# Attention and two feed-forward blocks on one core: the causal mask as a VectorE addition in PSUM, fewer products for the row maxima, and a new order

## The chip, the cores and the metric

The kernel runs on one core of a Trainium2 chip. Its engines work side by side, each through its own queue in order: TensorE (PE; its weight loads are PEld), VectorE (DVE), ScalarE (ACT), GpSimd (POOL) and SyncE (SP), which here only issues DMA transfers. Matrix products go to PSUM, eight banks of 512 float32 columns on 128 partitions. The metric is the device time of one execution in microseconds, lower is better.

## The reference

Three steps, all in float32, for 2 batches of 448 tokens and 12 heads of 64:

```python
scores = scale * np.matmul(q, k.transpose(0, 1, 3, 2))        # scale = 1/8
mask = np.triu(np.ones((seq, seq), dtype=bool), k=1)
scores = np.where(mask, -1000000000.0, scores)
scores = scores - np.max(scores, axis=-1, keepdims=True)
attn = np.exp(scores)
attn = attn / (np.sum(attn, axis=-1, keepdims=True) + 1e-09)
x = np.matmul(attn, v)                                        # heads joined: 896 x 768

h = x @ w_in                                                  # 896 x 1024
e = np.exp(h - h_max); sm = e / (np.sum(e) + 1e-09)           # per token
solu = h * sm
ln = (solu - mean) / np.sqrt(var + 1e-06) * g_ln
x = ln @ w_out                                                # 896 x 768

h = np.maximum(x @ w_in2, 0.0)                                # 896 x 2048
out = h * h @ w_out2                                          # 896 x 768
```

## The kernel before

**Products in two parts.** Every operand of a product is split into a high part, rounded to the fast format of TensorE, and a low part, the rest. A product is then three: high x high, low x high, high x low.

**Attention, pair by pair.** The 24 heads are worked as 12 pairs, one head on partitions 0 to 63, the other on 64 to 127, so that two products of 64 rows stand side by side. For pair i the steps are named by a short name and i:

- `load_r`, `H`, `L`: keys and queries come in; ScalarE makes the high part, GpSimd the low part.
- `S0a`, `S0b`, `S0c`: products of queries and keys for the row maxima alone, in one group of 448 keys, one of 336 and 112, one of 224. VectorE adds the mask MK and reduces them (`mxa`, `mxb`, `mxc`, line 298), and so frees the banks.
- `mT`, `row`, `rowd`: TensorE turns the maxima into rows, ScalarE copies them out, and two DMA transfers put them into one row a head of the tile MR (lines 306 to 326).
- `Sa`, `Sb`: the transposed scores, keys on partitions, queries in columns, only at and above the diagonal. The first half tile has key block 0 (448 queries, at column 64) and key block 3 (64 queries, at column 0); the second has blocks 1 (320, at 192) and 2 (192, at 0). To the three products come the row maxima, subtracted as a product of NEG1 and MR, and the mask, four products of ID (halves of the identity) and TR (0 or -1e30), lines 348 to 353. Pair 0 subtracts its maxima in another way (line 359).
- `ea1`, `eb1`: ScalarE's exponential of a whole half tile, into PP.
- `Ua`, `Ub`: products of PP with the values and a column of ones; `EA`, `EB` copy them out.
- `sums`, `recips`, `rcd`, `spread`, `norm`: the sums go through DMA, a reciprocal on VectorE, DRAM and back as `bc`; GpSimd multiplies.
- `x_hi`, `x_lo`: the parts of x for the next product, high on ScalarE, low on VectorE.

**The weights.** w_in comes as 64-bit floats, put together by three integer operations of VectorE over 1024 columns (`wf.0` to `wf.5`, lines 150 to 152), then split: high part on ScalarE (`wh`), low part on VectorE or GpSimd (`wl`).

**PSUM.** Half score tiles take two of four banks (a tile is given back after its exponential); the products for the maxima, the transposed maxima and U share the other four. A step takes the bank that was given back the longest time ago in the written order, and waits for it.

**What sets the order.** The string SEQ lists all steps up to the second block; each engine gets its instructions in that order and keeps it. `fl` steps are products that nobody reads. Behind attention come the steps of the first block (`h0` to `h6`, the layer norm, `T`, `y0`, `y1`) and the second block, which is not in SEQ.

Of the kernel before, what the change touches and what calls it, by code (L numbers as in the profile page):

```python
# [31 lines left out]
load_r.5 mT.2 Sa.1 row.2 EA.0 rowd.2 EB.0 load_v.2 S0a.3 ea1.1 S0b.3 sums.0 mxa.3 Sb.1 lq.9 lq.2 mxb.3 S0c.3 Sa.2 H.4
mxc.3 eb1.1 L.4 S0c.4 mT.3 ea1.2 mxc.4 Sb.2 recips.0 row.3 lq.3 S0b.4 eb1.2 rcd.0 Ua.1 mxb.4 load_v.3 rowd.3 S0a.4
Ub.1 mxa.4 spread.0 wf.0 load_r.6 Ua.2 lq.7 EA.1 H.5 mT.4 Sa.3 row.4 EB.1 norm.0 sums.1 S0b.5 load_v.4 ea1.3 Ub.2
mxb.5 rowd.4 L.5 load_r.7 x_hi.0 recips.1 Sb.3 EA.2 rcd.1 EB.2 S0c.5 sums.2 S0a.5 H.6 mxc.5 Sa.4 mxa.5 eb1.3 L.6 S0a.6
spread.1 mT.5 Sb.4 recips.2 lq.10 row.5 mxa.6 ea1.4 rcd.2 rowd.5 S0b.6 x_lo.0 H.7 Ua.3 mxb.6 load_r.8 norm.1 S0c.6
Ub.3 mxc.6 L.7 x_hi.1 spread.2 S0b.7 Sa.5 eb1.4 mxb.7 EA.3 EB.3 S0c.7 mT.6 mxc.7 Sb.5 wh.0 sums.3 x_lo.1 row.6 wl.0
ea1.5 S0a.7 rowd.6 Ua.4 H.8 load_v.5 norm.2 recips.3 load_r.9 mxa.7 eb1.5 rcd.3 Ub.4 lq.11 wf.1 mT.7 EA.4 Sa.6
load_v.6 EB.4 row.7 sums.4 S0c.8 ea1.6 Sb.6 spread.3 rowd.7 L.8 mxc.8 S0b.8 H.9 Ua.5 mxb.8 load_v.7 x_hi.2 eb1.6
x_lo.2 Ub.5 recips.4 wh.1 norm.3 rcd.4 load_r.10 S0a.8 Sa.7 mxa.8 L.9 EA.5 spread.4 x_hi.3 mT.8 S0a.9 EB.5 Sb.7 mxa.9  # L40
row.8 sums.5 ea1.7 load_r.11 x_lo.3 S0c.9 Ua.6 H.10 rowd.8 mxc.9 norm.4 eb1.7 load_v.8 recips.5 S0b.9 rcd.5 Ub.6 mxb.9
ld.5 wl.1 x_hi.4 mT.9 EA.6 Sa.8 row.9 EB.6 x_lo.4 sums.6 S0a.10 ea1.8 Sb.8 spread.5 L.10 mxa.10 load_v.9 rowd.9 S0b.10
H.11 Ua.7 mxb.10 ld.3 norm.5 S0c.10 Ub.7 mxc.10 recips.6 rcd.6 wf.2 mT.10 EA.7 Sa.9 row.10 eb1.8 S0b.11 EB.7 Sb.9
x_hi.5 spread.6 ea1.9 sums.7 L.11 mxb.11 Ua.8 load_v.10 rowd.10 x_lo.5 S0a.11 Ub.8 mxa.11 norm.6 recips.7 rcd.7 S0c.11
Sa.10 mxc.11 ld.4 wf.3 EA.8 eb1.9 mT.11 Ua.9 row.11 ea1.10 rowd.11 Sb.10 x_hi.6 spread.7 wh.3 Ub.9 wh.2 eb1.10 wl.2
Sa.11 EB.8 x_lo.6 sums.8 load_v.11 Sb.11 norm.7 ea1.11 h0.0 recips.8 wf.4 rcd.8 EA.9 Ua.10 eb1.11 x_hi.7 EB.9 h0.1
spread.8 sums.9 x_lo.7 wh.4 h1.0 wl.3 Ua.11 recips.9 norm.8 rcd.9 Ub.10 wf.5 h1.1 x_hi.8 spread.9 h0.2 h1.2 wl.4 wh.5
h0.3 EA.10 x_lo.8 EB.10 wl.5 h1.3 sums.10 h0.4 norm.9 recips.10 Ub.11 rcd.10 h1.4 EA.11 x_hi.9 spread.10 EB.11 x_lo.9
h0.5 sums.11 h1.5 mx.0 h2.0 norm.10 ex.0 recips.11 mx.1 rcd.11 load_g.0 h2.1 mu.0 x_hi.10 h2.2 spread.11 x_lo.10 sq.0
de.0 h2.3 ex.1 va.0 pw.0 h2.4 mu.1 norm.11 h2.5 h3.0 mx.2 x_hi.11 h3.1 fa.0 de.1 ln.0 x_lo.11 h3.2 lw.0 ex.2 h3.3 sq.1  # L50
de.2 mu.2 h4.0 va.1 sq.2 h3.4 va.2 lw.1 of.0 T.0 pw.2 pw.1 h3.5 Th.0 h4.1 fa.2 mx.3 h4.2 fa.1 ex.3 Tl.0 lw.2 h4.3 ln.2
# [809 lines left out]
```

## Time and profile before

| what | us |
|---|---|
| runs: 469.32, 469.99, 470.15 | median 469.99 |
| the profiled execution | 469.13 |
| its span, first to last instruction | 467.3 |
| PE busy | 458.8 (98%) |
| DVE busy | 267.4 (57%) |
| ACT busy | 165.8 (35%) |
| POOL busy | 134.4 (29%) |

The profile is one execution. Attention takes about the first 100 us; the first h product stands in the chain at 101.7 us. Busy shares are means over stages that differ much, so the rows below are taken by stretch. The end of a matmul is modelled; how long a group of matmuls holds the engine is read from the start of one group to the start of the next, as the chain has it.

### The profile page before, as it was taken

The page shows a single profiled execution, that of the slowest core. Times are in us where ns is not written, and L with a number is a line of the kernel's source. Part 1 is how long each engine was busy: PE and PEld are TensorE (multiplying, and loading weights), DVE is VectorE, ACT ScalarE, POOL GpSimd, SP SyncE. Part 2 cuts the span into 40 slices and gives each one's busy share as a digit, 9 for nine tenths or more (in the row PEclk, how much of TensorE's full clock was granted, in tenths as well). Part 3 has the DMA queues.
Part 4 walks back from the last instruction along what each step waited for, and adds up shares of the span by engine and source line. Part 5 has one row for each costly group of instructions (what it writes and reads, how often), then busy time and mean ns, then how long its engine had stood idle before and what let it go on. Part 6 is the DMA issues. An engine that isn't in the chain of part 4 may idle for free.

```text
span 467.3 us, 6795 instructions
## 1 busy us (share of the span) xinstructions
PE 458.8 (98%) x2659; PEld 410.0 (88%) x2659; DVE 267.4 (57%) x514; ACT 165.8 (35%) x225; POOL 134.4 (29%) x95
## 2 busy tenths in 40 slices
...
GB/s 265 152 157 139 114 165 219 123 125 39 23 103 320 0 182 157 2 0 1 0 69 135 74 130 106 97 135 74 129 104 100 136 74 131 199 122 135 79 59 118
DMA packets 41713, 52.48 MB, mean 112 GB/s; under 512 B 18257, under 2 KB 32337, under 8 KB 41297
## 3 DMA queue, kind: packets, MB, share of 16 engines
...
q8 instruction: 21, 0.34, 0.3%
q14 instruction: 12, 0.09, 0.1%
...
## 4 chain that ended last, share of the span: by engine, by line
PE 92%; DVE 5%; issue 1%; DMA 1%; POOL 1%; ACT 1%; SPq 0%; DVEq 0%; ACTq 0%; POOLq 0%
PE h L775 25%; PE o L804 25%; PE y L641 12%; PE h L494 12%; PE U L377 8%; PE s L345 4%; DVE JK L298 2%; PE mxp L283 2%; PE T L619 1%; DMA bc<-d 1%; PE s L353 1%; DVE wf L151 1%; POOL x L419 1%; PE fill L523 1%; PE mT L306 0%
## 5 line engine op out<-in xcount | busy, mean ns | idle before, releaser
L697 POOL TENSOR_TENSOR w<-wf,w 128x768 fp32r<-128x768 f32 x32 | 59.2, 1851 | 207.4 <-ACT w L694 207.4
L775 PE MATMUL h<-yT,w 128*128 128x448 f32 x576 | 116.9, 365 | 0.0
L804 PE MATMUL o<-w,g 128*128 128x384 f32 x672 | 116.7, 336 | 0.0
L804 PEld LDWEIGHTS o<-w,g 128*128 128x128 f32 x672 | 116.5, 188 | 0.0
L775 PEld LDWEIGHTS h<-yT,w 128*128 128x128 f32 x576 | 108.2, 188 | 8.6
L694 ACT CAST w<-wf 128x768 fp32r<-128x768 f32 x32 | 26.8, 837 | 140.9 <-DVE wf L152 95.7
L150 DVE TENSOR_SCALAR wf<-raw 128x768 int32<-128x768 int32 (+1 forms) x46 | 27.7, 602 | 82.8 <-DMA raw<-in_moe_w_out_dram 57.4
L494 PE MATMUL h<-w,xT 128*128 128x512 f32 x252 | 59.2, 393 | 0.0
L641 PE MATMUL y<-lnT,w 128*128 128x384 f32 (+1 forms) x288 | 58.9, 365 | 0.0
L641 PEld LDWEIGHTS y<-lnT,w 128*128 128x128 f32 x288 | 51.9, 188 | 5.9
L494 PEld LDWEIGHTS h<-w,xT 128*128 128x128 f32 x252 | 46.9, 188 | 9.6
L298 DVE CUSTOM_DVE_ANT_0 JK<-mxp,MK 112x336 bf16<-112x336 f32 (+2 forms) x96 | 40.0, 446 | 24.8 <-PE mxp L283 21.3
L151 DVE SCALAR_TENSOR_TENSOR wf<-raw,wf 128x768 int32<-128x768 int32 (+1 forms) x46 | 51.2, 1112 | 1.6
L377 PE MATMUL U<-PP,VR 128*128 128x448 f32 (+1 forms) x192 | 48.6, 399 | 0.8 <-DVE mx L298 0.7
L152 DVE SCALAR_TENSOR_TENSOR wf<-raw,wf 128x768 int32<-128x768 int32 (+1 forms) x46 | 48.3, 1049 | 1.6
L377 PEld LDWEIGHTS U<-PP,VR 128*128 128x128 f32 x192 | 32.0, 190 | 16.1 <-issue 9.6
L419 POOL TENSOR_TENSOR x<-E,bc 64x448 f32<-64x448 f32 x24 | 30.5, 1270 | 40.8 <-DVE xT L431 23.3
L272 POOL TENSOR_TENSOR LO<-r,HI 128x896 fp32r<-128x896 f32 x12 | 26.9, 2245 | 14.6 <-ACT HI L268 14.2
L368 ACT ACTIVATE PP<-s 128x1024 f32<-128x1024 f32 x24 | 24.4, 1018 | 7.2 <-PE s L353 5.3
L761 DVE TENSOR_TENSOR relu<-h,relu 128x896 f32<-128x896 f32 x16 | 17.5, 1092 | 14.6 <-ACT relu L760 14.6
L389 ACT ACTIVATE E<-U,SE 128x448 f32<-128x448 f32 x24 | 14.6, 630 | 24.1 <-POOL x L419 15.1
L763 ACT CAST g<-relu 128x896 fp32r<-128x896 f32 x16 | 15.1, 941 | 18.6 <-DVE relu L761 18.6
...
## 6 DMA issues: line engine op xcount, KB each, us to landing
...
```

The lines of the kernel that those rows point to most:

```text
L150: nc.vector.tensor_scalar(xi, hw, 3, 0x3FFFFFFF, ALU.logical_shift_left, ALU.bitwise_and)
L151: nc.vector.scalar_tensor_tensor(xi, hw, -0x40000000, xi, ALU.bitwise_and, ALU.bitwise_or)
L152: nc.vector.scalar_tensor_tensor(xi, lw, 29, xi, ALU.logical_shift_right, ALU.bitwise_or)
L272: eng.tensor_tensor(LO[i % 3][:, :, 0:S], kq_raw.pop(i), f(HI[i % 3][:, :, 0:S]), ALU.subtract)
L298: nc.vector.tensor_tensor_reduce(JK[t], bs[h][0:JP, o : o + nk], MK[:, S - nk :], 1.0, NEG, ALU.add, ALU.max, mx[i][:, 4 * h + t : 4 * h + ...
L377: nc.tensor.matmul(UB[i][h][:, q0:S], VR[i % 3][:, t, h, :], PP[(2 * i + a) % NPP][:, h, o : o + nq], start=t == 0, stop=t == 2,)
L419: nc.gpsimd.tensor_tensor(x[D * h : D * h + D], e[0:D, h], bc[:, h], ALU.mult)
L494: nc.tensor.matmul(b[:, half, :], xT[c][s][:, t * P : t * P + P], W1[c][:, w, 512 * half : 512 * half + 512], start=(c == 0 and s == 0 and ...
L641: nc.tensor.matmul(b[:, ci, 0:n], WO[fi][:, w, c * P : c * P + P], M["lnT"][a][s][:, fi, :], start=(fi == 0 and w == 0 and s == 0), stop=( ...
L697: nc.gpsimd.tensor_tensor(W2[n][:, 1], w_f["2", n], f(W2[n][:, 0]), ALU.subtract)
L775: nc.tensor.matmul(b[:, a, 0:HT], W2[fi][:, w, c * P : c * P + P], yT[c][s][:, HT * a : HT * a + HT], start=(c == 0 and w == 0 and s == 0) ...
L804: nc.tensor.matmul(ob, G[fi + e][s][:, P * t : P * t + P], w, start=(fi + e == 0 and r == 0), stop=(fi + e == NF2 - 1 and r == 2),)
```

## The change

The four mask products of each half score tile are gone, and with them the tile ID. Instead VectorE adds the mask TR to the tile in PSUM, in place, before the exponential: a new step, `ka` for the first half (2 x 192 columns) and `kb` for the second (2 x 2 x 128 columns). The tile MR is 64 columns wider and holds the last 64 maxima of a head a second time in front of the others, so that the maxima of the first half are subtracted in one product of 512 columns a head; for that, `rowd` issues four transfers instead of two. All low parts of x are GpSimd's. PP has five buffers instead of four, one `fl` group is gone, and SEQ is written anew as a whole.

```diff
-NPP = 4
-XLO_POOL = ()
+NPP = 5
+XLO_POOL = (0, 1, 2, 3, 4, 5, 6, 7, 8, 9, 10, 11,)
...
 SEQ = """
-load_r.0 load_v.0 fl.0 fl.1 fl.2 H.0 load_r.1 fl.3 lq.4 load_v.1 L.0 S0c.0 S0a.0 fl.4 mxa.0 fl.5 mxc.0 fl.6 S0b.0 H.1
+load_r.0 fl.0 fl.1 fl.2 H.0 load_r.1 fl.3 lq.0 L.0 S0b.0 fl.4 mxb.0 fl.5 S0c.0 S0a.0 mxc.0 fl.6 H.1 load_r.2 fl.7
...
-            MR = [qk.tile([P, S], F32R, name=f"MR{i}") for i in range(3)]
+            MR = [qk.tile([P, D + S], F32R, name=f"MR{i}") for i in range(3)]
...
-            TR = per.tile([P, 2, 320], F32R, name="TR")
-            ID = per.tile([P, 2, P], F32R, name="ID")
+            TR = per.tile([P, D + P], F32, name="TR")
...
-                for h in range(2):
-                    nc.vector.tensor_copy(ID[D * h : D * h + D, j], ident[D * j : D * j + D])
-            nc.vector.tensor_copy(TR[D:P], f(TR[0:D]))
+            nc.gpsimd.memset(TR, 0.0)
+            for o, n in ((0, D), (D, P)):
+                ap = TR[:, o : o + n]
+                nc.gpsimd.affine_select(ap, ap, [[1, n]], ALU.is_ge, HUGE, base=0, channel_multiplier=-1)
...
                 for h in range(2):
                     nc.sync.dma_start(
-                        f(MR[i % 3][D * h : D * h + 1]).rearrange("o (t p) -> o t p", p=JP),
+                        f(MR[i % 3][D * h : D * h + 1, D:]).rearrange("o (t p) -> o t p", p=JP),
                         f(m2[4 * h : 4 * h + 4]),
                     )
+                    nc.sync.dma_start(f(MR[i % 3][D * h : D * h + 1, 0:D]), f(m2[4 * h + 3 : 4 * h + 4, JP - D :]))
...
-                for K, Q in ((HIk, HIq), (LOk, HIq), (HIk, LOq), (None, MR[i % 3])):
+                for K, Q in ((HIk, HIq), (LOk, HIq), (HIk, LOq)):
...
-                for j in range(2):
+                for o, x, n in () if i in mr else (((0, 0, D + S),), ((192, D + P, S - P), (0, D + 2 * P, S - 2 * P)))[a]:
                     for h in range(2):
                         r = slice(D * h, D * h + D)
-                        b = s[:, h, 0 : 192 * a + 192].rearrange("p (a c) -> p a c", c=192)[:, :, 0 : 192 - 64 * a]
-                        x = TR[r, j, 64 * a : 192 + 128 * a].rearrange("p (a c) -> p a c", a=1 + a)
-                        nc.tensor.matmul(b, ID[r, j], x, start=False, stop=j == 1 and i not in mr)
+                        nc.tensor.matmul(
+                            s[:, h, o : o + n], NEG1[r], MR[i % 3][r, x : x + n], start=False, stop=o == 0
+                        )
...
+            def causal(n):
+
+                if n % 2 == 0:
+                    x, y = sb[n][:, :, 0 : D + P], TR.unsqueeze(1).broadcast_to((P, 2, D + P))
+                else:
+                    x = sb[n][:, :, 0:384].rearrange("p h (b c) -> p h b c", c=192)[:, :, :, 0:P]
+                    y = TR[:, D:].unsqueeze(1).unsqueeze(1).broadcast_to((P, 2, 2, P))
+                nc.vector.tensor_tensor(x, x, y, ALU.add)
```

Three places show what stands on an engine now; line numbers of the changed kernel are a few higher or lower than those of the kernel before.

On TensorE, the first half score tile of pair 1 (HI and LO are parts of keys and queries, s is the tile), before:

```order
L345 MATMUL s<-LO_128,HI_125 128x448 x2
L345 MATMUL s<-LO_128,HI_125 128x64 x2
L345 MATMUL s<-MR_131,NEG_133 128x448 x2
L345 MATMUL s<-MR_131,NEG_133 64x64 x2
L353 MATMUL s<-TR,ID 128x192 x4
```

and in the changed kernel:

```order
L336 MATMUL s<-LO_128,HI_125 128x448 x2
L336 MATMUL s<-LO_128,HI_125 128x64 x2
L344 MATMUL s<-MR_131,NEG_133 128x512 x2
L300 MATMUL mT<-ident,mx 8x112
L379 MATMUL U<-PP_144,VR_140 128x320
```

The two products of the maxima (448 and 64 columns) are one of 512, the mask's four are gone, and the next step follows.

On VectorE, around the second conversion of w_in (`wf.1`, three operations on wf), from the last maxima of pair 7 (JK_139 is the 448-key group) to the next one, before:

```order
L298 ISA JK_139,mx<-mxp,MK 112x448
L298 ISA mx 112x1
L150 TENSOR_SCALAR wf<-raw 128x1024
L151 SCALAR_TENSOR_TENSOR wf<-raw,wf 128x1024
L152 SCALAR_TENSOR_TENSOR wf<-raw,wf 128x1024
L298 ISA JK_137,mx<-mxp,MK 112x224
L298 ISA mx 112x1
L298 ISA JK_137,mx<-mxp,MK 112x224
```

and in the changed kernel:

```order
L292 ISA JK_139,mx<-mxp,MK 112x448
L292 ISA mx 112x1
L151 TENSOR_SCALAR wf<-raw 128x1024
L152 SCALAR_TENSOR_TENSOR wf<-raw,wf 128x1024
L153 SCALAR_TENSOR_TENSOR wf<-raw,wf 128x1024
L367 TENSOR_TENSOR s<-s,TR 128x2x192
L292 ISA JK_139,mx<-mxp,MK 112x448
L292 ISA mx 112x1
L292 ISA JK_139,mx<-mxp,MK 112x448
L292 ISA mx 112x1
L367 TENSOR_TENSOR s<-s,TR 128x2x2x128
```

Behind the conversion now stand an addition of the mask (pair 6, first half), the 448-key maxima of pair 8 and a second addition, where the 224-key maxima of pair 8 stood.

On SyncE's queue, from the rows of maxima of pair 1 (MR_131) to those of pair 2 (MR_132; m holds the rows, raw is w_in, r keys and queries), before:

```order
L323 DMA MR_131<-m_338 1x4x112 x2
L478 DMA raw<-in_moe_w_in_dram 128x512 x2
L223 DMA r<-in_kq_dram 128x896
L323 DMA MR_132<-m_432 1x4x112 x2
L226 DMA VR_142<-in_v_dram 128x8x64
```

and in the changed kernel:

```order
L317 DMA MR_131<-m_338 1x4x112
L321 DMA MR_131<-m_338 1x16x4
L317 DMA MR_131<-m_338 1x4x112
L321 DMA MR_131<-m_338 1x16x4
L481 DMA raw<-in_moe_w_in_dram 128x512 x2
L224 DMA r<-in_kq_dram 128x896
L317 DMA MR_132<-m_398 1x4x112
L321 DMA MR_132<-m_398 1x16x4
L317 DMA MR_132<-m_398 1x4x112
L321 DMA MR_132<-m_398 1x16x4
```

Each pair's row transfers are four where there were two; what stands between them is the same here.

## Rows read from the trace of the kernel before

**Rows 1.** Busy us (x instructions) of each engine by stretch, TensorE's granted clock

```profile
12.00:99.00 87.00, 84.56 (x709) 65.70 (x707) 61.02 (x200) 47.70 (x71) 42.31 (x25) 1.00 0.54 156
99.00:464.00 365.00, 365.00 (x1916) 337.54 (x1912) 197.05 (x273) 113.36 (x149) 83.45 (x51) 1.00 0.31 96
```

**Rows 2.** Who TensorE waited for, 12 to 110 us: total, times, longest

```profile
PE mT L306 <- DVE mx L298: 1.0, 3, 0.5
PE U L377 <- DVE mx L298: 0.7, 1, 0.7
PE s L345 <- ACT PP L368: 0.6, 1, 0.6
```

**Rows 3.** Who VectorE waited for, 5 to 96 us: total, times, longest

```profile
DVE JK L298 <- PE mxp L283: 21.3, 19, 3.0
```

**Rows 4.** The chain that ended last: start us, length us, what (x instructions)

```profile
86.91 2.09 PE U L377 x8
...
89.60 1.92 PE U L377 x8
...
91.82 1.18 PE s L345 x16
...
98.77 1.37 PE s L345 x15
100.14 0.28 PE s L353 x4
...
101.47 0.25 PE s L353 x4
101.72 1.59 PE h L494 x6
...
121.64 20.42 PE h L494 x90
```

**Rows 5.** The timeline of the start: start us, us, engine, line, what [idle before]

```profile
3.85 0.87 DVE L254 CAST ID<-ident 64x128 fp32r<-64x128 f32 x4
...
4.73 0.49 DVE L255 CAST TR<-TR 64x640 fp32r<-64x640 f32 x1
...
6.86 0.56 DVE L298 CUSTOM_DVE_ANT_0 JK<-mxp,MK 112x448 bf16<-112x448 f32 x1
...
13.40 0.62 DVE L298 CUSTOM_DVE_ANT_0 JK<-mxp,MK 112x448 bf16<-112x448 f32 x1
...
14.85 0.26 PE L306 MATMUL mT<-ident,mx 112*8 112x112 f32 x1 [0.33 <-DVE mx L298]
```

**Rows 6.** VectorE by shape, 195 to 240 us: busy us, mean ns, idle before

```profile
L670 DVE TENSOR_TENSOR yT<-y,yT 128x512 fp32r<-128x512 f32 x6 | 4.2, 692 | 20.8 <-ACT yT L669 20.8
L670 DVE TENSOR_TENSOR yT<-y,yT 128x384 fp32r<-128x384 f32 x6 | 3.3, 557 | 3.3 <-ACT yT L669 3.3
```

**Rows 7.** VectorE by shape, 0 to 96 us: the low parts of x

```profile
L431 DVE TENSOR_TENSOR xT<-x,xT 128x448 fp32r<-128x448 f32 x6 | 5.0, 840 | 0.0
```

**Rows 8.** The timeline around two conversions of w_in

```profile
57.38 2.44 POOL L272 TENSOR_TENSOR LO<-r,HI 128x896 fp32r<-128x896 f32 x1
57.88 3.01 DVE L151 SCALAR_TENSOR_TENSOR wf<-raw,wf 128x1024 int32<-128x1024 int32 x1
...
92.72 0.69 DVE L150 TENSOR_SCALAR wf<-raw 128x1024 int32<-128x1024 int32 x1
...
93.44 1.23 DVE L151 SCALAR_TENSOR_TENSOR wf<-raw,wf 128x1024 int32<-128x1024 int32 x1
```

**Rows 9.** The timeline of the row of maxima and of small transfers

```profile
22.88 1.21 SPq L323 DMA_DIRECT2D MR<-m  x2
...
75.18 0.24 ACT L311 CAST m<-mT 8x112 fp32r<-8x112 f32 x1 [0.32 <-PE mT L306]
...
99.42 0.58 SPq L394 DMA_DIRECT2D sc<-E  x1
...
101.48 0.20 DVE L400 RECIPROCAL sr<-sc 112x8 f32<-112x8 f32 x1 [1.74 <-DMA sc<-E]
```

More of the change, by code (lines that the diff above doesn't have):

```diff
@@ L32 @@
[L32 to L51, printed above, removed]
@@ new lines @@
+mxa.0 load_v.0 fl.8 lq.1 L.1 S0c.1 fl.9 mxc.1 mxr.0 fl.10 S0a.1 S0b.1 mxa.1 Sa.0 mxb.1 H.2 load_r.3 L.2 ka.0 S0a.2
+mT.1 mxa.2 Sb.0 lq.2 row.1 ea1.0 rowd.1 lq.8 S0b.2 H.3 Ua.0 mxb.2 lq.3 L.3 load_r.4 kb.0 S0c.2 Sa.1 eb1.0 mxc.2 mT.2
+ka.1 Ub.0 row.2 rowd.2 ea1.1 load_v.1 S0a.3 EA.0 Sb.1 load_r.5 mxa.3 EB.0 sums.0 S0b.3 H.4 kb.1 S0c.3 Sa.2 mxc.3 eb1.1
+L.4 mxb.3 load_v.2 S0c.4 Sb.2 mxc.4 mT.3 recips.0 row.3 S0b.4 rcd.0 H.5 Ua.1 mxb.4 rowd.3 L.5 lq.4 ka.2 load_r.6 kb.2
+S0a.4 ea1.2 load_v.3 Ub.1 mxa.4 spread.0 eb1.2 wf.0 mT.4 EA.1 Sa.3 lq.5 row.4 EB.1 S0b.5 sums.1 Sb.3 Ua.2 mxb.5 H.6
@@ new lines @@
+load_v.4 rowd.4 norm.0 ka.3 recips.1 S0a.5 ea1.3 kb.3 Ub.2 rcd.1 load_r.7 mxa.5 x_hi.0 x_lo.0 S0c.5 EA.2 load_v.5 Sa.4
+mxc.5 eb1.3 spread.1 L.6 mT.5 S0c.6 Sb.4 row.5 mxc.6 EB.2 wh.0 ka.4 sums.2 S0a.6 Ua.3 rowd.5 mxa.6 ea1.4 lq.6 kb.4
+norm.1 H.7 S0b.6 recips.2 eb1.4 Ub.3 mxb.6 rcd.2 load_r.8 x_hi.1 wl.0 S0c.7 EA.3 Sa.5 EB.3 spread.2 x_lo.1 mT.6 sums.3
+ka.5 Sb.5 row.6 mxc.7 L.7 rowd.6 ea1.5 S0b.7 Ua.4 lq.7 mxb.7 norm.2 recips.3 kb.5 rcd.3 S0a.7 Ub.4 lq.9 mxa.7 eb1.5
+load_r.9 H.8 wf.1 mT.7 Sa.6 spread.3 row.7 EA.4 EB.4 S0a.8 x_hi.2 Sb.6 sums.4 load_v.6 x_lo.2 ka.6 Ua.5 rowd.7 H.9
@@ new lines @@
+mxa.8 norm.3 ea1.6 kb.6 S0c.8 Ub.5 recips.4 eb1.6 mxc.8 rcd.4 load_v.7 L.8 x_hi.3 S0b.8 Sa.7 EA.5 mxb.8 EB.5 wh.1
+sums.5 S0b.9 x_lo.3 mT.8 mxb.9 spread.4 Sb.7 row.8 load_r.10 L.9 rowd.8 S0a.9 ka.7 Ua.6 kb.7 load_v.8 ea1.7 recips.5
+mxa.9 rcd.5 eb1.7 norm.4 lq.10 Ub.6 H.10 load_r.11 S0c.9 Sa.8 wl.1 mxc.9 EA.6 spread.5 x_hi.4 EB.6 S0c.10 ka.8 mT.9
+lq.11 Sb.8 row.9 mxc.10 ea1.8 rowd.9 x_lo.4 S0b.10 Ua.7 sums.6 mxb.10 H.11 ld.3 L.10 kb.8 S0a.10 Sa.9 eb1.8 mxa.10
+norm.5 Sb.9 recips.6 ka.9 rcd.6 load_v.9 mT.10 Ub.7 row.10 load_g.0 wf.2 ea1.9 rowd.10 Ua.8 EA.7 spread.6 EB.7 x_hi.5
@@ new lines @@
+sums.7 kb.9 x_lo.5 ld.4 S0b.11 Ub.8 load_v.10 mxb.11 eb1.9 norm.6 S0a.11 Sa.10 mxa.11 recips.7 L.11 EA.8 S0c.11 rcd.7
+Sb.10 mxc.11 x_hi.6 mT.11 kb.10 Ua.9 row.11 EB.8 x_lo.6 rowd.11 ka.10 wh.2 spread.7 wf.3 ea1.10 sums.8 Ub.9 ld.5
+eb1.10 Sa.11 norm.7 recips.8 Ua.10 ka.11 rcd.8 load_v.11 ea1.11 Sb.11 wl.2 x_hi.7 EA.9 h0.0 EB.9 x_lo.7 kb.11 sums.9
+eb1.11 h0.1 spread.8 wf.4 wh.3 Ua.11 norm.8 recips.9 Ub.10 rcd.9 h1.0 wl.3 EA.10 spread.9 wh.4 h1.1 x_hi.8 EB.10 Ub.11
+x_lo.8 sums.10 norm.9 h0.2 recips.10 h1.2 rcd.10 wf.5 EA.11 EB.11 h0.3 x_hi.9 sums.11 h2.0 x_lo.9 wh.5 h1.3 recips.11
@@ new lines @@
+rcd.11 wl.4 spread.10 h3.0 wl.5 h1.4 h0.4 norm.10 h0.5 h1.5 mx.0 x_hi.10 spread.11 x_lo.10 h2.1 mx.1 ex.0 h2.2 mu.0
+ex.1 norm.11 h2.3 mu.1 sq.0 h2.4 de.0 va.0 x_hi.11 pw.0 h2.5 x_lo.11 h3.1 mx.2 lw.0 h3.2 de.1 ex.2 h3.3 mu.2 h3.4 fa.0
+ln.0 of.0 lw.1 h3.5 sq.1 T.0 h4.0 va.1 mx.3 pw.1 h4.1 fa.1 ex.3 h4.2 of.1 lw.2 Th.0 h4.3 oh.0 ln.1 ol.0 h4.4 sq.2 Tl.0
+h4.5 oh.1 mu.3 lw.3 h5.0 of.2 sq.3 T.1 h5.1 Th.1 mx.4 h5.2 ol.1 ex.4 lw.4 h5.3 de.2 de.3 va.2 h5.4 va.3 pw.2 mu.4 pw.3
+h5.5 fa.2 fa.3 ln.2 Tl.1 h6.0 sq.4 mx.5 T.2 ln.3 of.3 h6.1 ex.5 T.3 Th.2 h6.2 mu.5 oh.3 h6.3 l2.2 Tl.2 Th.3 l2.1 lw.5
@@ L57 @@
+oh.2 h6.4 Tl.3 sq.5 de.4 h6.5 de.5 ol.2 y0.0 mx.6 va.4 ex.6 of.4 y0.1 ol.3 oh.4 ol.4 y0.2 va.5 lw.6 mu.6 pw.5 l2.0
+pw.4 of.5 y0.3 de.6 oh.5 fa.4 of.6 lw.7 ln.4 y0.4 sq.6 fa.5 oh.6 ol.5 T.4 va.6 ol.6 pw.6 y0.5 Th.4 ln.5 Tl.4 fa.6 of.7
+ln.6 T.5 y0.6 Th.5 Tl.5 oh.7 ol.7 T.6 y0.7 Th.6 Tl.6 f2.0 y1.0 yo.2 g2.0 yo.1 o2.0 f2.1 y1.1 y1.2 yp.1 yp.0 g2.1 yo.0
 o2.1 yp.2
```

24 lines of the change are left out of this document (5 added, 19 removed).

## The prediction

> **What bounds the kernel now.** I read the views in this order: busy time by stretch, who waited for whom, the chain that ended last, then single rows around the score groups. From 99 to 464 us TensorE is busy all 365 us; from 12 to 99 us, where the attention pairs run, it is busy 84.6 of 87 us, at a granted clock of 1.00 in both [rows 1]. In that first stretch it waits for others about 2.3 us in all, nearly always for VectorE's maxima [rows 2]. So a microsecond of TensorE work that disappears is a microsecond of the span, as long as the engines that feed it keep up. VectorE is the one to watch: it is busy 61.0 of the same 87 us [rows 1], and most of its 26 us of idleness is 21.3 us of waiting for maximum products [rows 3], spare time before and something it can lose.
>
> **The change part by part, on TensorE.** The four mask matmuls behind each half score tile go. In the chain they hold the engine 0.28 us (first half) and 0.25 us (second half) from their first start to the next work [rows 4]; twelve of each are 12 x 0.28 + 12 x 0.25 = 6.4 us. They sit on the path, so I count all of it.
>
> In the first half the row of maxima was subtracted by 448 and 64 columns a head and is now one product of 512. No row shows a 512-column product on 64 rows. Four products cost 1.37 us in the first half (448 + 64) and 1.18 in the second (320 + 192), so 0.34 and 0.30 each; a 512-column product of the h stage takes 20.42 / 90 = 0.23 us [rows 4]. The saving is therefore between 0 (a single pair overlaps its weight loads no better) and 0.34 - 0.23 = 0.11 us; I take 0.06, the middle. Eleven pairs have it: 0.6 us, bounds 0 and 1.2.
>
> **The start.** VectorE no longer builds the identity halves and the second mask copy, 0.87 + 0.49 us in front of its first maximum at 6.86 us [rows 5]. From there to the first transposition, 14.85 us, it is the engine that TensorE ends up waiting for, and TensorE fills the time with products that nobody reads [rows 5]. So the chain moves up by 1.36 us, less 0.2 for the wider maxima tiles that it clears. I take 1.0 us; bounds 0 (if the first loads land no earlier and become what is late) and 1.4. The dropped filler group costs and saves nothing: it stood inside this wait.
>
> **What VectorE gets.** 24 additions in PSUM, of 384 and 512 elements. No row shows VectorE writing PSUM. The nearest rows read one PSUM and one SBUF operand at just these sizes and write SBUF: 0.56 and 0.69 us [rows 6]. From below, 384 of the 448 columns that a maximum pass reads from PSUM in 0.62 us [rows 5] are 0.53; from above, 0.84 is what an operation of 448 columns takes on average where others disturb it [rows 7]. I take the mean of the nearest rows, 0.62, 15.0 us in all (13 to 20). It gives up the low parts of x, 0.84 us each [rows 7], six of them within this stretch: 5.0 us. So VectorE has 61.0 + 15.0 - 5.0 = 71.0 us to do where TensorE, after the savings, has about 79. That fits, but only in the right order: 8 us of spare time where there were 26. What hides each addition is the distance on TensorE between a score tile and the U product that reads it: by the order, 6 to 13 us of TensorE work in every pair but the first, against 0.6 for the add and the exponential behind it.
>
> The cover is thin where VectorE converts w_in, because the additions and maxima queue behind three long operations. The second conversion is the clearest place. Between the maximum product for pair 7 (448 keys) and the product that needs the banks of pair 8's 448-key maximum, TensorE has a U half of 1.92, two score halves of 1.31 and 1.18, a U half of 2.09 and about 0.4 of small work: 6.9 us [rows 4]. VectorE has in that time one maximum (1.3 to 1.45 us from 13.40 to the transposition, [rows 5]), the conversion, an addition and another maximum. With an undisturbed conversion of 0.69 + 1.23 and, for the third operation, as much again, 3.15 us [rows 8], that is 6.4 us, no wait. With one of its operations stretched from 1.23 to 3.01, as [rows 8] has it, it is 8.2 us: a wait of 1.3 us. The first conversion has the same shape with a little less behind it, a wait of 0 to 1.2 us.
>
> **The low parts of x on GpSimd.** Twelve operations of some 1.2 us (half of a 2.44 us one on twice the columns, [rows 8]) on an engine with room. By themselves they cost nothing. What they may do is disturb VectorE: the middle operation of the second conversion starts at 57.88 beside a GpSimd operation that runs from 57.38 to 59.82, and ends 1.07 us after it, 3.01 us where the same operation undisturbed takes 1.23 [rows 8]. By the Trainium skill, page "SBUF — State Buffer", section "Who interferes with whom", this is a lock and not sharing: a VectorE instruction with two SBUF inputs and a GpSimd one that reads SBUF do not run together, the later waits the whole of the earlier out; one with at most one SBUF input is free of it. The trace agrees for the conversion. By that rule the additions, with one operand in PSUM, pay nothing, and each moved low part can hold up a conversion, which speaks against this half of the change.
>
> **The queue of row transfers.** The first 64 columns of the new maxima tile need a copy of their own: four transfers a pair where there were two. Each takes the queue 0.6 us (two in 1.21), and a small transfer is usable 2.06 us after its issue starts (99.42 to 101.48) [rows 9]. From the transposition to the copied row are 0.6 us (0.24 behind 0.32 of waiting), so the last of four is there 0.6 + 3 x 0.6 + 2.06 = 4.5 us after it. TensorE has, in the tightest three pairs (2, 9 and 11), 4.0 us of other work plus about 0.9 us of that tile's own products: 4.9. The cover holds by 0.4 us. Should something stand ahead in the queue, these pairs wait a few tenths.
>
> **Sum.** 6.4 + 0.6 + 1.0 = 8.0 us gained. For new waits at conversions, at the maximum products and at the tight pairs I take 2.0 us beyond the 2.3 there were; that is the middle of none (both conversions undisturbed) and 4 (both disturbed, 2.5, and half a microsecond in three pairs). Net 6.0 us. The profiled execution took 469.13 us (span 467.3 and 1.8 around it), which gives 463.1; the median of the runs lies 0.86 us above the profiled one, so 464.0 us. In the stages behind attention only the order changes, and TensorE never waits there now [rows 1].
>
> **Rivals.**
> 1. The conversions are hit: low parts on GpSimd land beside the conversions as the operation of 57.38 did, each of the four before the last score tile lasts 1.8 us longer, and half of this stands in TensorE's way beyond the forecast: 4 x 1.8 / 2 = 3.6 us, 467.6. (The page named above has this as a rule.) For it: [rows 8]. Against: leaving VectorE, the low parts also stop being blocked themselves (0.84 on average, where the add of 384 takes 0.56, [rows 6, 7]), and GpSimd had room before.
> 2. Slower: VectorE becomes the engine that sets the end of the attention stretch. It works in order, and its wait for products is 21.3 us [rows 3]; if those waits stay, since each product still waits for a bank that VectorE frees, it needs 71.0 + 21.3 = 92.3 us where the stretch took 87. That is 5.3 us more, less 1.0 from the start: about 474 us. It decides from 16 us of VectorE idleness on (71 + 16 = 87). Against: the waits in [rows 3] are largely those of an engine that is ahead, and they shrink as it has more to do.
> 3. The four row transfers come late: 22 more issues of 0.6 us are 13 us of the queue. If each of eleven pairs then waits 0.9 us, 10 us go and the result is 464.0 + 10 = 474 us, slower too. It needs the row copy or the queue to be about 1.3 us late in every pair; eight pairs have over 0.5 us more cover than the tight ones.
> 4. The additions replace the mask one for one (the change does not do what it says): TensorE, freed of 6.4 us, waits as long for the adds, and only start and merged product remain: 469.99 - 1.0 - 0.6 = 468.4. Against: the 6 to 13 us of cover.
>
> **How the numbers follow.** Forecast 0.62 (its own range 461 to 466.5), rival 1 0.17, rival 2 0.09, rival 3 0.04, rival 4 0.08. A measurement tells this kernel from no change at about 0.2%, 0.9 us: faster is below 469.1. The forecast, rival 1 and half of rival 4 lie there, 0.83; no difference is the other half, 0.04; slower are rivals 2 and 3, 0.13. The range for 8 in 10 reaches from 460.8 (no wait at all, the start's upper bound) to 469.0, which takes in rivals 1 and 4.
>
> **What would show it.** The mask matmuls gone and the 512-column product at about 0.28 us a pair; the first transposition near 13.7 us; the additions at 0.56 and 0.69; the first h product some 6 us earlier than 101.7 [rows 4]. Wrong would be: TensorE waits for VectorE or ScalarE over 6 us in the attention stretch, conversions of 5 us and more throughout, or score tiles waiting for a transfer of the maxima row. A wait in the stages behind would mean that their order, which I took as harmless, is not.

## The result, and the profile after

The changed kernel is slower: 476.51 us (four runs, 474.63 to 478.71) beside 469.65 for the kernel before (469.09 to 470.15), a ratio of 1.0148 [1.0102, 1.0194]. The forecast was 464.0, range 460.8 to 469.0: wrong in its sign. The profiled execution took 478.71 us, its span is 476.9, 9.6 more than before, and its mean granted clock is 0.981 where it was 1.000.

The stretches of the changed kernel, as in [rows 1]: busy us (x instructions) of PE, PEld, DVE, ACT, POOL, then the granted clock, DMA share and GB/s.

```profile
12.00:99.00 87.00, 81.00 (x568) 60.39 (x567) 59.24 (x209) 43.89 (x63) 43.83 (x30) 0.92 0.52 138
99.00:464.00 365.00, 362.46 (x1884) 332.54 (x1882) 198.50 (x273) 116.62 (x153) 93.62 (x59) 1.00 0.32 99
```

The same by shorter stretches:

```profile
12.00:40.00 28.00, 27.70 (x216) 20.99 (x213) 20.25 (x79) 13.46 (x19) 8.19 (x4) 1.00 0.49 130
40.00:60.00 20.00, 17.42 (x101) 12.57 (x102) 12.59 (x45) 9.59 (x14) 13.15 (x10) 0.74 0.40 104
```

Read the first line of this block and then the second: up to 40 us nothing is wrong, from 40 to 60 TensorE is idle 2.58 us and, worse, runs at a mean clock of 0.74. TensorE is idle 6.0 us from 12 to 99 us where it was 2.4, and 2.5 us behind 99 where it was 0. Over the whole span the idle time is 476.9 - 462.8 = 14.1 us against 467.3 - 458.8 = 8.5: 5.6 more. The clock costs, by an estimate from its mean, 476.9 x (1 - 0.981) = 9.1 us. Together 14.7, of which 9.6 are seen; the rest, 5.1, is by this estimate work that really went. So in this execution nearly two thirds of what was lost are not waits at all, they are what follows the waits. It is the longest of the four: the other three, at mean clocks of 0.989, 0.993 and 0.993, took 476.58, 474.63 and 476.44 us, and by the same estimate the clock cost them 5.2, 3.3 and 3.3 us. So the waits weighed more there.

Who TensorE waited for, 12 to 130 us (total, times, longest), against [rows 2]:

```profile
PE mxp L277 <- DVE mx L292: 4.9, 6, 2.4
PE h L497 <- ACT E L391: 1.9, 1, 1.9
PE s L344 <- DMA MR<-m: 1.0, 1, 1.0
PE mT L300 <- DMA raw<-in_moe_w_in_dram: 0.7, 1, 0.7
```

And VectorE in the same stretch, against [rows 3]:

```profile
DVE JK L292 <- PE mxp L277: 17.1, 15, 2.8
DVE sr L402 <- DMA sc<-E: 16.0, 7, 7.7
```

TensorE waits for VectorE's maxima, while VectorE is only busy 59 us of 87. VectorE is not overloaded; it stands at line 402, the reciprocal of the sums, waiting for a transfer: 16.0 us, where the kernel before has 4.2 in the same view. This is the row to follow, but not by its total. Nearly half of it is one long wait near the end, and a faster kernel of the experiments below, e1, has it too (changed kernel, then e1):

```profile
123.31 0.20 DVE L402 RECIPROCAL sr<-sc 112x8 f32<-112x8 f32 x1 [7.66 <-DMA sc<-E]
...
111.66 0.20 DVE L402 RECIPROCAL sr<-sc 112x8 f32<-112x8 f32 x1 [8.02 <-DMA sc<-E]
```

The total less this longest wait is 8.3 us here, and 7.0 in e13, 4.3 in e5, 3.5 in e1 and 2.2 in e9: the order of their times.

The transfer of the sums of pair 1 starts in SyncE's queue at 35.16 us (start, length of the issue):

```profile
29.38 0.67 SPq L317 DMA_DIRECT2D MR<-m  x1
30.11 0.56 SPq L321 DMA_DIRECT2D MR<-m  x1
30.71 0.62 SPq L317 DMA_DIRECT2D MR<-m  x1
31.38 0.52 SPq L321 DMA_DIRECT2D MR<-m  x1
...
35.16 0.55 SPq L396 DMA_DIRECT2D sc<-E  x1
```

The queue has no pause there: nine issues stand end to end from 29.38 us to the sums, and the four row transfers take 2.37 us of that. The chain that ended last runs through them, and then through 5.79 us of the sums' transfer. The sums are used 5.8 us after their issue starts, and this is what VectorE and TensorE then do (start, length, idle before and its releaser):

```profile
40.98 0.20 DVE L402 RECIPROCAL sr<-sc 112x8 f32<-112x8 f32 x1 [3.58 <-DMA sc<-E]
41.10 0.67 DVE L367 TENSOR_TENSOR s<-s,TR 128x512 f32<-128x512 f32 x1
41.68 0.61 DVE L292 CUSTOM_DVE_ANT_0 JK<-mxp,MK 112x448 bf16<-112x448 f32 x1
...
42.36 0.55 PE L277 MATMUL mxp<-HI 64*128 64x224 f32 x1 [2.39 <-DVE mx L292]
```

VectorE waits 3.58 us for the sums with an addition of the mask and the 448-key maxima queued behind; these maxima hold the PSUM bank that TensorE wants next, and TensorE is idle 2.39 us. Its clock afterwards, in stretches around that moment (columns as above):

```profile
38.00:40.00 2.00, 1.97 (x10) 1.35 (x8) 0.00 (x0) 0.95 (x2) 0.00 (x0) 1.00 1.13 205
40.00:42.00 2.00, 0.00 (x0) 0.00 (x0) 1.02 (x3) 0.00 (x0) 1.89 (x2) 1.00 0.39 67
42.00:44.00 2.00, 1.42 (x8) 1.15 (x9) 1.52 (x7) 1.60 (x3) 1.32 (x2) 0.54 0.67 181
44.00:48.00 4.00, 4.00 (x29) 3.37 (x29) 1.28 (x7) 2.11 (x4) 2.80 (x3) 0.50 0.56 148
...
52.00:54.00 2.00, 2.00 (x11) 1.30 (x11) 0.79 (x5) 0.60 (x2) 1.32 (x2) 0.90 0.78 212
```

Until 42 us it is granted 2.4 GHz; from then, after an idle stretch of two microseconds, 1.2 GHz, for ten microseconds of nearly unbroken work (48 to 52 us reads as 44 to 48), before it rises again. So a wait of 2.4 us cost about 5 more behind it (half of ten, an estimate). There are two more such places, of which this is the next:

```profile
63.69 0.69 DVE L151 TENSOR_SCALAR wf<-raw 128x1024 int32<-128x1024 int32 x1 [1.55 <-DMA raw<-in_moe_w_in_dram]
...
65.68 2.05 DVE L153 SCALAR_TENSOR_TENSOR wf<-raw,wf 128x1024 int32<-128x1024 int32 x1
...
68.79 0.37 PE L277 MATMUL mxp<-HI 64*128 64x224 f32 x1 [1.40 <-DVE mx L292]
```

At 63.69 a conversion waits 1.55 us for its weights, another late transfer, its third operation takes 2.05 us where the second took 1.23, and then TensorE waits for the maxima behind it. At 126.32 the first block's products wait (the second row of TensorE's waits, 1.9 us) for a PSUM bank that ScalarE's copy of U frees, and the copy for a buffer that GpSimd's multiplication frees. From there the chain that ended last goes back over GpSimd's other work, two low parts of x among it (1.73 and 1.12 us), and two `bc` transfers to the row transfers of the last pair, 101.65 to 103.63. But e1 and e9 have 0.8 and 1.0 us of the same wait, so the added transfers are not all of it.

### The profile page after: what moved, and what is told of

The parts are those of the page before. It is cut to its first block, busy times and chain, and to the rows that moved or that the text cites. A ratio compares the mean times of both kernels' runs of the same rounds, so it can differ in the third digit from the quotient of the medians.

```text
span 476.9 us, 6621 instructions
## 1 busy us (share of the span) xinstructions
PE 462.8 (97%) x2539; PEld 409.2 (86%) x2539; DVE 268.1 (56%) x521; ACT 166.6 (35%) x225; POOL 144.4 (30%) x103
## 4 chain that ended last, share of the span: by engine, by line
PE 82%; DMA 6%; POOL 4%; SPq 4%; issue 2%; ACT 1%; DVE 1%; ACTq 0%; POOLq 0%; DVEq 0%
PE h L778 24%; PE o L807 24%; PE y L644 12%; PE h L497 10%; PE U L379 3%; DMA bc<-d 2%; POOL x L421 2%; PE s L336 2%; PE fill L526 2%; PE mxp L277 1%; SPq L317 1%; PE T L622 1%; DMA d<-sr 1%; DMA sc<-E 1%; SPq L321 1%
## 5 line engine op out<-in xcount | busy, mean ns | idle before, releaser
L497 PE MATMUL h<-w,xT 128*128 128x512 f32 x252 | 61.1, 401 | 1.9 <-ACT E L391 1.9
L497 PEld LDWEIGHTS h<-w,xT 128*128 128x128 f32 x252 | 47.9, 192 | 12.3 <-ACT E L391 2.3
L379 PE MATMUL U<-PP,VR 128*128 128x448 f32 (+1 forms) x192 | 51.6, 417 | 0.0
L152 DVE SCALAR_TENSOR_TENSOR wf<-raw,wf 128x768 int32<-128x768 int32 (+1 forms) x46 | 47.3, 1029 | 1.6
L153 DVE SCALAR_TENSOR_TENSOR wf<-raw,wf 128x768 int32<-128x768 int32 (+1 forms) x46 | 47.3, 1028 | 1.6
L379 PEld LDWEIGHTS U<-PP,VR 128*128 128x128 f32 x192 | 33.7, 200 | 16.8 <-issue 11.8
L421 POOL TENSOR_TENSOR x<-E,bc 64x448 f32<-64x448 f32 x24 | 29.0, 1208 | 28.8 <-DMA bc<-d 27.9
L266 POOL TENSOR_TENSOR LO<-r,HI 128x896 fp32r<-128x896 f32 x12 | 25.2, 2100 | 16.0 <-ACT HI L262 15.8
L277 PE MATMUL mxp<-HI 64*128 64x336 f32 (+3 forms) x96 | 17.0, 366 | 4.9 <-DVE mx L292 4.9
```

What stands on the lines that cost most here:

```text
L152: nc.vector.scalar_tensor_tensor(xi, hw, -0x40000000, xi, ALU.bitwise_and, ALU.bitwise_or)
L153: nc.vector.scalar_tensor_tensor(xi, lw, 29, xi, ALU.logical_shift_right, ALU.bitwise_or)
L379: nc.tensor.matmul(UB[i][h][:, q0:S], VR[i % 3][:, t, h, :], PP[(2 * i + a) % NPP][:, h, o : o + nq], start=t == 0, stop=t == 2,)
L421: nc.gpsimd.tensor_tensor(x[D * h : D * h + D], e[0:D, h], bc[:, h], ALU.mult)
L497: nc.tensor.matmul(b[:, half, :], xT[c][s][:, t * P : t * P + P], W1[c][:, w, 512 * half : 512 * half + 512], start=(c == 0 and s == 0 and ...
```

## Experiments

Theory Q: the 22 added row transfers delay everything that SyncE issues behind them (sums, weights, keys and queries), and VectorE, in order, passes the delay on. Rivals: the additions load VectorE too much (V); GpSimd's low parts are the harm, to VectorE or by GpSimd's own lateness (G; the recorded expectations call it P); the new order as a whole is bad (O). In e4 and e13 the added copies go to columns that nobody reads, and e14 adds part of the mask twice, which leaves the result as it is. Comparisons with e1 and with the changed kernel are of medians; the kernel before had 469.36 to 469.65 beside them.

### e1_two_rows: two row transfers a pair, the rest as changed

```diff
-MR = [qk.tile([P, D + S], ...
+MR = [qk.tile([P, S], ...
-nc.sync.dma_start(f(MR[i % 3][D * h : D * h + 1, 0:D]), f(m2[4 * h + 3 : 4 * h + 4, JP - D :]))
-s[:, h, o : o + n], NEG1[r], MR[i % 3][r, x : x + n]           # one product of 512
+s[:M, h, o : o + nq], NEG1[r, 0:M], MR[i % 3][r, q0 : q0 + nq]  # 448 and 64
```

> The changed kernel with two row transfers a pair and the row subtracted by 448 and 64 columns again; order, additions and GpSimd's share stay. Theory Q (22 more transfers crowd the transfer queue, so sums and loads come late, VectorE stands at the reciprocal and TensorE's clock falls): VectorE's 16.0 us of waiting for sums falls under 6, time 467 to 470. Theory O (the new order itself puts the sums behind bulk loads and the reciprocals ahead of additions): waits stay over 12 us, time 474 to 478. Theory P (GpSimd's low parts): as O, 474 to 478.

465.52 us, 0.9915 [0.9900, 0.9930]: 11 us faster than the changed kernel and 4 faster than the kernel before. Its clock is 1.00 in every stretch. The same place in it: the rows take two issues, the sums leave 1.64 us earlier, and TensorE waits 0.80.

```profile
28.60 1.31 SPq L317 DMA_DIRECT2D MR<-m  x2
...
33.52 0.59 SPq L396 DMA_DIRECT2D sc<-E  x1
...
39.15 0.20 DVE L402 RECIPROCAL sr<-sc 112x8 f32<-112x8 f32 x1 [2.21 <-DMA sc<-E]
...
40.53 0.37 PE L277 MATMUL mxp<-HI 64*128 64x224 f32 x1 [0.80 <-DVE mx L292]
```

The added transfers, with the one product of 512 columns that they served, are the cause of the sign. The additions, GpSimd's low parts and the new order are still in this kernel and it is faster. It came out better than Q had expected (467 to 470), while VectorE's wait for the sums stayed at 11.5 us and did not fall under 6: 8.0 of it is the long wait near the end.

### e13_three_rows: e1 with one added transfer a pair

```diff
+if h == 0:
+    nc.sync.dma_start(f(MR[i % 3][0:1, S:]), f(m2[3:4, JP - D :]))
```

> The kernel with two row transfers a pair and one more on SyncE's queue (a copy of 64 maxima that nobody reads): three transfers. Theory Q, each 0.6 us of issue in front of sums and loads counts by itself: half of the way from 465.5 to 476.5, so 468 to 473. Rival: the loss comes at a step, only where several delays meet: 465 to 467, all of it with the fourth transfer.

471.74 us, 1.0046 [1.0023, 1.0069], 6.2 above e1 where two added transfers cost 11.0. TensorE's idle time from 12 to 130 us is 6.7 us (3.8 in e1, 8.6 with two), the clock 0.91 from 40 to 60 us (0.74 with two). VectorE's wait for the sums is 16.0 us as with two added, and shows the dose only without the longest wait (7.0, between 3.5 and 8.3). So the loss grows with each transfer, and not through the product, since nobody reads the copy.

### e4_before_four_rows: the kernel before with the two added transfers

```diff
+nc.sync.dma_start(f(MR[i % 3][D * h : D * h + 1, 0:D]), f(m2[4 * h + 3 : 4 * h + 4, JP - D :]))
```

> The kernel before with two more row transfers a pair (the second copy of the last 64 maxima is written and not read); all else as before. Theory Q: each costs 0.6 us of the queue in the tight pairs, 472 to 477 with clock dips. Theory O: 469 to 471, the queue has room in that order.

474.40 us, 1.0110 [1.0091, 1.0129]: 5 us, without any of the other edits. The path is another one here: the reciprocals' way back (`bc`) is late for GpSimd, whose multiplication frees the buffer that ScalarE copies U into, whose PSUM bank TensorE wants.

```profile
83.03 3.25 POOL L420 TENSOR_TENSOR x<-E,bc 64x448 f32<-64x448 f32 x2 [3.47 <-DMA bc<-d]
...
86.32 0.63 ACT L390 ACTIVATE E<-U,SE 128x448 f32<-128x448 f32 x1 [7.05 <-POOL x L420]
...
87.00 0.47 PE L283 MATMUL mxp<-HI 64*128 64x336 f32 x3 [1.76 <-ACT E L390]
```

### e5_rows_on_act and e9_all_rows_on_act: rows issued by ScalarE

e5 is the changed kernel with its two added transfers issued by ScalarE, e9 is e1 with both row transfers there:

```diff
-nc.sync.dma_start(f(MR[i % 3][D * h : D * h + 1, ...
+nc.scalar.dma_start(f(MR[i % 3][D * h : D * h + 1, ...
```

> The changed kernel with the two extra row transfers a pair issued from ScalarE's queue instead of SyncE's; four transfers and the 512-column product stay. If it is the issue time on SyncE's queue that delays sums and loads (theory Q): 465 to 470, VectorE waits for sums under 13 us. If it is the transfers themselves (more small packets in the DMA engines): 474 to 478 as in the changed kernel. If ScalarE has no room for 1.2 us of issues a pair: over 470 with TensorE waiting for exponentials.

> The kernel with two row transfers a pair (465.5 us), both issued from ScalarE's queue right behind the copy of the row; SyncE's queue loses another 1.2 us a pair. If the queue is still what makes the sums late: VectorE's wait for sums under 8 us, 462 to 464.8. If what is left is the time the bulk loads take in the DMA engines: 465 to 467, VectorE's wait about 11.5 us as now.

e5: 467.40 us, 0.9953 [0.9938, 0.9967]. The same 44 transfers, the same bytes, half of them on another queue, and 9.1 us less: of the 11.0 that e1 gains, most is the place in SyncE's queue and not the transfers themselves. The 1.9 us that e5 stays above e1 (467.40 and 465.52) can be the transfers or their issue by ScalarE. e9: 464.68 us, 0.9894 [0.9877, 0.9912], the lowest median and ahead of both kernels; its interval overlaps that of e1, so the 0.8 us between the two are not shown. VectorE's wait for the sums is 10.5 us, not under 8 as expected, 8.3 of it the long one. All that TensorE waits for in it, 12 to 130 us:

```profile
PE h L497 <- ACT E L391: 1.0, 1, 1.0
PE mxp L277 <- DVE mx L292: 0.4, 2, 0.2
```

### e10_rows_sums_on_act: e9 with the sums issued by ScalarE too

```diff
-nc.sync.dma_start(c, ee[i][D : D + 1] ...
+nc.scalar.dma_start(c, ee[i][D : D + 1] ...
```

> As the kernel before it, and the transfers of the sums too from ScalarE's queue, so that none of them stands behind bulk loads in SyncE's queue. If the queue position is what is left: under 464. If ScalarE's 1.8 us a pair of issues, in order in front of its exponentials, cost more than they save: 466 to 470.

470.53 us over all ten runs, which reach from 467.6 to 475.9; the ratio, 1.0020 [1.0003, 1.0037], leaves out the two longest. Worse than e9, not better. Its profile is of the longest run, so I read no cause from it. It stays open.

### e6_recips_later and e7_sums_first: two cures by order

e6 is the changed kernel with `recips` of pairs 0 to 8 (and `rcd`, in part `spread`) three VectorE steps later; e7 is e1 with bulk loads put behind the sums, pairs 0 to 5. Around pair 0 in e6, pair 1 in e7 (steps of SEQ; "..." stands for steps that stay):

```diff
-mT.3 recips.0 row.3 S0b.4 rcd.0 H.5
+mT.3 row.3 S0b.4 H.5
...
-load_r.6 kb.2 S0a.4
+load_r.6 kb.2 recips.0 rcd.0 S0a.4
```

```diff
-lq.4 ka.2 load_r.6 kb.2 S0a.4 ea1.2 load_v.3 Ub.1
+ka.2 kb.2 S0a.4 ea1.2 Ub.1
...
-lq.5 row.4 EB.1 S0b.5 sums.1 Sb.3
+row.4 EB.1 S0b.5 sums.1 lq.4 load_r.6 load_v.3 lq.5 Sb.3
```

> The changed kernel with each of the first nine reciprocals three VectorE steps later in the written order (and the transfers that follow it). If the path from late sums to TensorE is VectorE standing in order at the reciprocal, its wait for sums falls below 8 us and the time to 468 to 473. If late loads and rows of maxima are the path: waits move, time stays at 474 to 478. If the multiplication on GpSimd becomes late instead: slower than 478.

> The kernel with two row transfers (465.5 us) and, in the written order, the bulk loads that stood in front of the sums of pairs 0 to 5 right behind them. If sums land late because the bulk loads in front of them fill the DMA engines: VectorE's wait for sums falls from 11.5 to under 7 us and the time to 462 to 465. If it is only the queue's length: 465 to 467, no change.

Both missed. e6: 498.54 us, 1.0608 [1.0580, 1.0636]. VectorE no longer waits for sums, but the reciprocals come later, so the chain of e4 is late, GpSimd first, TensorE last:

```profile
POOL x L421 <- DMA bc<-d: 44.1, 8, 8.3
...
PE mT L300 <- ACT E L391: 7.7, 2, 7.1
```

e7: 475.25 us, 1.0131 [1.0105, 1.0157], 9.7 worse than e1. VectorE's wait for sums does fall, from 11.5 to 9.5 us, or from 3.5 to 1.4 without the longest; but ScalarE's for keys and queries grows from 3.5 to this:

```profile
ACT HI L262 <- DMA r<-in_kq_dram: 19.9, 6, 5.9
```

So the reciprocal has deadlines on both sides, and what comes earlier on SyncE's queue makes something else late: in these two tries a new order gave the queue no room.

### e2_xlo_dve, e8_two_rows_xlo_dve, e12_before_xlo_pool: the low parts of x

e2 is the changed kernel, e8 is e1, each with low parts on VectorE; e12 is the kernel before with them on GpSimd:

```diff
-XLO_POOL = (0, 1, 2, 3, 4, 5, 6, 7, 8, 9, 10, 11,)
+XLO_POOL = ()
```

> The changed kernel with the low parts of x on VectorE again, all else kept. Theory P (GpSimd's extra work holds up the multiplication, and with it the transfers that wait for its buffers): 467 to 471. Theories Q and O: 475 to 479, no better, since VectorE only gets 7 us more to do.

> The kernel with two row transfers (465.5 us) and the low parts of x on VectorE again. If moving them to GpSimd is worth something once the queue is free (VectorE has 15 us of additions now): 467 to 471. If it is worth nothing or harms, as the conversions are disturbed by GpSimd: 463 to 465.5.

> The kernel before with the low parts of x on GpSimd and nothing else. The forecast's second case (GpSimd's operations hold the conversions up): 471 to 474. If moving them only frees VectorE: 467 to 469.5. No difference is likely where VectorE has 26 us of spare time: 469 to 470.5.

e2: 476.16 us, 1.0139 [1.0117, 1.0162], as the changed kernel. This alone does not settle G, since e2 also gives VectorE more to do; but e1 keeps GpSimd's low parts and is faster than the kernel before, so G falls as the cause of the sign. e8: 471.31, 1.0039 [1.0024, 1.0054], 5.8 above e1; in its profile 5.2 of 6.1 us are the lower clock (469.7 x (1 - 0.989)). e12: 469.30, 0.9993 [0.9981, 1.0006], nothing. The move is worth nothing alone, is needed beside the additions, and cannot be seen beside the four row transfers. One place in e8 where TensorE waits has again an operation of VectorE with others behind it:

```profile
41.24 2.04 DVE L433 TENSOR_TENSOR xT<-x,xT 128x448 fp32r<-128x448 f32 x1 [0.22 <-ACT xT L429]
...
44.27 0.34 PE L300 MATMUL mT<-ident,mx 112*8 112x112 f32 x1 [1.62 <-DVE mx L292]
```

### e3_old_order_adds: the additions in the order before

The kernel before with the additions, each directly ahead of its exponential, two rows, low parts on VectorE:

```diff
-ea1.0
+ka.0 ea1.0
...
-eb1.0
+kb.0 eb1.0
```

> The additions alone: mask matmuls out, additions in, each written directly before its exponential in the order of the kernel before, two row transfers, low parts of x on VectorE, four PP buffers. Theory O: most of the 6.4 us of TensorE work comes back as time, 463 to 466. Theory V (VectorE has no room for 15 us more with low parts too, whatever the order): 470 to 478, with TensorE waiting over 8 us for maxima or additions.

488.35 us, 1.0404 [1.0386, 1.0421]: the additions alone, in the old order, lose 19 us. ScalarE's exponentials wait for VectorE, and TensorE for the score banks that they free (12 to 130 us):

```profile
ACT PP L370 <- DVE s L367: 40.1, 17, 5.1
...
PE s L335 <- ACT PP L370: 9.1, 4, 4.6
```

### e11_new_order_no_adds: the new order with the mask on TensorE

The new order without `ka` and `kb`, low parts on GpSimd, five PP, and score products and mask as before, seen here against the changed kernel:

```diff
-ka.0 S0a.2
+S0a.2
...
-nc.vector.tensor_tensor(x, x, y, ALU.add)
+nc.tensor.matmul(b, ID[r, j], x, start=False, stop=j == 1 and i not in mr)
```

> The new order, five PP buffers, GpSimd's low parts and two row transfers with the mask still as four products on TensorE: the new order without the additions. If the additions' gain (6.4 us of TensorE work) is what the kernel with two row transfers has over the kernel before, less what they make VectorE late: 467 to 472. If the order alone is the gain: 465 or less.

468.53 us, 0.9983 [0.9962, 1.0005], no difference that can be told: O falls. The order gains nothing by itself; beside e3 it is what makes room for the additions. It also sizes the mask, beside e9, in the chain of pair 6. With mask products (e11; start, length):

```profile
57.91 1.37 PE s L345 x16
59.28 0.28 PE s L353 x4
...
59.78 1.00 PE s L345 x16
60.78 0.25 PE s L353 x4
```

and without (e9):

```profile
57.42 1.05 PE s L335 x12
58.47 0.34 PE s L344 x4
...
59.02 0.74 PE s L335 x12
59.76 0.26 PE s L344 x4
```

The first half takes 1.65 us against 1.40, the second 1.25 against 1.00: 0.25 each, by this one pair 24 x 0.25 = 6.0 us in all. Of these e1 shows only 468.53 - 465.52 = 3.0 in the medians; in its profile TensorE is idle 3.8 us from 12 to 130 where e11 has 0.1.

### e14_second_add_twice: e1 with the second addition made twice

```diff
+if n % 2:
+    nc.vector.tensor_tensor(x, x, y, ALU.add)
```

> The kernel with two row transfers a pair, and the addition of every second half tile made twice (the masked scores only get more negative): 12 x 0.69 = 8.3 us more for VectorE, nothing else. If VectorE's time is what has eaten about half of the 6.4 us of mask products (theory V): 468 to 474 with more TensorE waits for maxima. If VectorE still has room in this order: 465 to 467.

470.37 us, 1.0019 [1.0001, 1.0037], 4.9 above e1 for 12 x 0.69 = 8.3 us of VectorE. In its profile TensorE is idle only 0.2 us more than in e1 (9.5 and 9.3), but its mean clock is 0.992, which is 3.7 of the 4.1 us between the two spans. VectorE's time is not free in this order, though in e1 it is busy only 66 of the 87 us from 12 to 99. That is where the difference between 6.0 and 3.0 us can go; V is right by a part, but it does not make the kernel slower than before.

## Why the prediction was wrong

**The step that failed is "The queue of row transfers".** It priced 22 more issues by what they do to the row itself: "the cover holds by 0.4 us". That was nearly so: the wait of score products for the row was 1.0 us, once. What stands behind the row in the same queue was not counted, the sums above all, nor the engine that waits for them: VectorE's reciprocal, with the additions and maxima of other pairs in order behind it. Nor do the 2.06 us from issue to use hold in that stretch: for the sums of pair 1 it is 5.8. e1, e13 and e5 show the queue (11.0 us for two transfers a pair, 6.2 for one, 9.1 back by another queue). How the 11 us divide among sums, weights and keys is not shown. Two of the prediction's own signs came: from 12 to 130 us TensorE waited 6.8 us for VectorE and ScalarE, and one score tile waited for its row.

**A term that was missing: TensorE's clock.** Every wait was priced at its own length. In the profile the waits are 5.6 us more and the lower clock behind them about 9; in the other three runs the clock is 3 to 5.

**Rivals.** Rival 3 named the cause, the transfers, and about the size (474), but by rows coming late in each pair, which they did not. Rival 2 had the side and VectorE, but from too much work: over the whole span VectorE is busy 268.1 us where it was 267.4, and e1, with the same work, is faster. Rival 4 did not happen: e9 against e11 shows the mask's time gone from TensorE. Rival 1 happened, but smaller. The conversions of the changed kernel in 0 to 105 us, with the additions in the same view (busy us, mean ns, idle before):

```profile
L367 DVE TENSOR_TENSOR s<-s,TR 128x512 f32<-128x512 f32 x11 | 7.6, 690 | 0.6 <-PE s L344 0.6
...
L367 DVE TENSOR_TENSOR s<-s,TR 128x384 f32<-128x384 f32 x11 | 6.2, 561 | 0.9 <-PE s L344 0.6 <-PE mxp L277 0.3
L152 DVE SCALAR_TENSOR_TENSOR wf<-raw,wf 128x1024 int32<-128x1024 int32 x4 | 5.7, 1432 | 0.1
...
L151 DVE TENSOR_SCALAR wf<-raw 128x1024 int32<-128x1024 int32 x4 | 3.6, 892 | 1.5 <-DMA raw<-in_moe_w_in_dram 1.5
```

and of e2, which has the same order and the low parts on VectorE:

```profile
L152 DVE SCALAR_TENSOR_TENSOR wf<-raw,wf 128x1024 int32<-128x1024 int32 x4 | 4.9, 1226 | 0.1
...
L151 DVE TENSOR_SCALAR wf<-raw 128x1024 int32<-128x1024 int32 x4 | 3.2, 798 | 1.5 <-DMA raw<-in_moe_w_in_dram 1.5
```

A conversion is 0.89 + 1.43 + 1.43 (line 153 like 152) = 3.75 us, and in e2 0.80 + 1.23 + 1.22 = 3.25: the low parts on GpSimd cost half a microsecond a conversion, not 1.8. Two of the eight long operations were stretched, to 2.05 us at 65.68 and 2.04 at 102.60, each beside a low part of x on GpSimd (64.69 to 66.65 and 101.97 to 103.56). The first operation, with one input, was stretched too, to 1.50 at 101.06, beside a GpSimd operation until 102.01. The one at 65.68 stands in front of TensorE's second wait; e2 without it is no faster. (The kernel before has 4.77 in the same view, in another order.)

**Terms that held.** The additions take 0.56 and 0.69 us, as [rows 6] gave them. The mask is 6.0 us, read from one pair, where 6.4 were taken.

**Terms that were mis-sized.** The product of 512 columns takes 0.31 us from its start to the next work (63.62 to 63.93 in the changed kernel) where 448 and 64 take 0.34 (e9): 0.03 a pair, 0.3 us and not 0.6, for two transfers a pair. The first transposition starts at 14.52 us, not 13.7; it was 14.85 [rows 5]. That is 0.3 us, but two maximum products of pair 2 (14.07 to 14.52) now stand in front of it and a group of mask products does not, so what the start alone gave is not shown. New waits, taken as 2.0 us, are of that order only where the queue is relieved: e1 has 1.4 more TensorE idle time than the kernel before from 12 to 130 us, e9 0.9 less. With 464.68 us, e9 lands near the 464.0, but by smaller gains and smaller waits than the sum had.
